# Attention and two MLPs in one kernel: a new order of issue with its own keys for block 1, a fifth `y` buffer, and the output staged in `of`

## The chip, the cores and the metric

One core of one Trainium2 chip (trn2). The metric is device time in microseconds (us). The kernel before takes 1407.87 us, the median of 3 runs (1406.32 to 1409.04).

## The reference

```python
# depthwise softmax-weighted window over 7 positions, 8 heads of 24 channels
w = softmax(weight_gen, axis=-1)                 # (2, 4096, 8, 7), + 1e-9 in the sum
out = einsum('bshk,bskhg->bshg', w, windows(x))  # x (2, 4096, 192), zero-padded by 6
x = out.reshape(8192, 192)
# first MLP
h = x @ w_in                                     # 192 -> 2048
x = (h * sigmoid(h)) @ w_out                     # 2048 -> 192
# second MLP, with a rational activation
h = x @ w_in2
P = a0 + a1 * h + a2 * h * h + a3 * h * h * h
Q = 1 + abs(b0) * abs(h) + abs(b1) * h * h
out = (P / (Q + 1e-6)) @ w_out2
```

The weights come as 64-bit floating-point words, which the kernel itself turns into fp32 high and low parts. All arithmetic is fp32, each product of two matrices being five matmuls over high and low parts.

## The kernel before, in words

The 8192 tokens are cut into 16 blocks of 512 (`NB`). A block goes through three stages: the attention (`M`, `p`, `r`, `a` for each of 4 groups of tokens, and the DMA `AD`), which ends with the transposition `T` into an `h` tile in PSUM and the split `XH0`, `XL0`; **unit 1**, eight times (u = 0 to 7) through the first MLP; and **unit 2**, eight times through the second.

A step of unit 1 is `A`u, ten matmuls into an `h` tile (128x1024, L516); on ScalarE `S`u, the SiLU in place (L553), and `H`u, the high part `g1h` (L557); on VectorE `L`u, the low part `g1l` (L561); then `C`u, ten matmuls from `g1h` and `g1l` into the accumulator (L537 to L541). After `C`7 come `EC` (a copy of half the accumulator into `of`, under the name `e`), `EM` (two matmuls, L577), and the split `XH1` (L489), `XL1` (L493).

A step of unit 2 is `B`u, ten matmuls into an `h` tile; on ScalarE `U`u (`t`, L592) and `V`u (`y`, L596), which both read the `h` tile; on VectorE `u`u (L602) and `w`u (L605), which read it again, and `Y`u (L611); on ScalarE `N`u (L616, Ln) and `G`u (L619, Sigmoid); on VectorE `g`u (L622); `h`u, the high part `g2h`, on POOL, ScalarE or VectorE (a helper, L215, L217, L219); `l`u, the low part `g2l` (L632), on VectorE or POOL; then `D`u, ten matmuls. After `D`7 come `FC` (the accumulator into `of`), `FT` (a transposition into an `h` tile), `FE` (from there to SBUF) and `O`, the DMA to the output (L667).

There are two `h` tiles, shared by `A`, `B`, `T` and `FT`: 18 uses for each block. A use can start when the readers of the use before the last are done. The framework also makes two engines that read one PSUM tile wait for each other, in the order in which they are issued, though both only read: a `V` that is issued between `u` and `w` waits for `u`, and `w` for `V`.

Which order the engines issue in is set by a table, `KEYS`: `Plan.op` gives each operation a key, and `Plan.order` sorts all operations by it; each engine runs its own in that order. A middle block's key is the table's value plus `b * PERIOD`. The first and the last block have keys of their own (`z` and `e` ahead of the name). `ENGINES` says which of the possible engines an operation runs on. Unit 2 of one block is interleaved with unit 1 of the next. At the start 28 chunks of weights are prepared (names `q`: `l` a DMA, `a` on ScalarE, `1` to `4` and mostly `x` on VectorE, L329 to L382), and three further parts of the softmax weights (`s1` to `s3`), which go to DRAM and come back block by block (`AW`, into `aw`).

ScalarE's functions need tables: `S` (SiLU), `N` (Ln) and `G` (Sigmoid) each another one, and the program has an ACT_TABLE_LOAD wherever one follows another; copies, `U` and `V` need none.

Of the kernel before, what the change touches and what calls it, by code (L numbers as in the profile page):

```python
# [37 lines left out]
KEYS = """
    cn:-2654.87 q0O0l:-1091.22 q0O2l:-1019.12 q0O0a:-846.22 q0A0l:-814.6 q0O2a:-791.41 q0A0a:-787.86 q0O01:-777.66
    q0O02:-773.39 q0O03:-728.14 q0O21:-683.64 q0B0l:-641.23 q0O04:-622.79 q0O22:-558.4 q0B0a:-553.51 q0B01:-551.38  # L40
    q0O0h:-534.54 q0O23:-490.66 q0A01:-489.63 q0O24:-458.65 q0A1l:-456.85 q0A02:-443.96 q0O2h:-432.99 cl:-416.6
    q0A1a:-414.24 s0l:-411.67 q0O0x:-411.37 q0A03:-410.2 s0m:-410.01 q0A04:-404.48 zX:-403.47 q0A0h:-401.08 ca:-383.3
    q0O1l:-377.93 s0e:-364.89 q0A11:-364.45 q0B02:-363.26 q0A0x:-362.65 q0O1a:-361.6 q0A2l:-354.79 q0O2x:-345.81
    q0B03:-316.92 q0A12:-309.71 q0B04:-303.11 s0n:-287.19 q0A2a:-276.83 q0B0d:-276.41 q0O11:-275.19 q0B0h:-271.54
    q0A13:-270.4 zM0:-265.19 q0O12:-257.47 q0A21:-246.3 q0A14:-238.64 zp0:-238.19 q0A22:-237.38 zr0:-229.4
    q0A23:-224.88 za0:-219.64 q0O13:-215.26 zM1:-214.13 q0A24:-200.03 q0O6l:-191.2 q0A3l:-175.29 q0A1h:-175.16
    q0A1x:-172.73 q0A3a:-168.08 zp1:-167.7 q0B1l:-164 q0A31:-160.72 q0O6a:-160.16 zr1:-157.97 q0O61:-156.06
    za1:-153.62 q0O62:-150.5 zM2:-148.24 q0O14:-147.91 zp2:-143.67 q0A32:-141.33 q0A2h:-139.04 zr2:-130.1
    q0B0x:-129.28 X:-122.84 za2:-121.15 q0O1h:-119.09 q0O63:-116.78 q0O3l:-114.33 zM3:-113.33 q0B1a:-108.33
    q0O1x:-107.5 zp3:-105.83 q0A33:-104.78 AW:-103.75 zr3:-103.7 M0:-102 q0B11:-99.99 p0:-99.17 q0O64:-98.62 r0:-95.49  # L50
    q0O3a:-95.08 za3:-94.88 q1A0l:-93.71 q0B12:-93.54 q0A34:-92.42 a0:-91.77 q0O31:-91.43 q0O6h:-90.26 M2:-89.49
    q0A2x:-89.37 q0B13:-87.76 zAD:-87.54 q0O32:-85.82 zT:-85.5 zXH0:-84.82 p2:-84.81 r2:-82.87 q0B14:-81.83 s1l:-79.62
# [674 lines left out]
```

## Time and profile before

| | us |
|---|---|
| median of 3 runs | 1407.87 (1406.32 to 1409.04) |
| the profiled execution's own time | 1408.39 |
| its span, first to last instruction | 1406.6 |
| TensorE (PE) busy | 1247.3 (89%) |
| VectorE (DVE) busy | 1144.8 (81%) |
| ScalarE (ACT) busy | 1044.6 (74%) |
| GpSimd (POOL) busy | 586.3 (42%) |

A block's period is read from one `EM` to the next: the sixteen `EM` start at 114.25, 202.64, 286.44, 366.81, 448.46, 528.88, 609.24, 689.59, 769.99, 851.63, 932.01, 1012.36, 1092.76, 1173.06, 1251.98 and 1328.33 us. A period without softmax work is about 80.4 us from `EM` of block 2 on, and one with `s2` or `s3` in it 81.6.

### The profile page before, as it was taken

Reading aid. Unit: us, or ns where it says so; the run is one execution under the profiler, and the core shown is the slowest. Engines: PE = TensorE matmul, PEld = TensorE weight load, DVE = VectorE, ACT = ScalarE, POOL = GpSimd, SP = SyncE. Lnnn points to the kernel's source line nnn. Section 1 sums busy time; section 2 is a strip of 40 time slices with the busy share of each in tenths; the row PEclk is TensorE's granted clock in tenths of the full one; section 3 lists DMA queues with packets and bytes.
Section 4 is the critical chain, followed back from the end, with each engine's and each line's share of the span. In section 5 each row is a group of like instructions: output and inputs, shape, how many; then the busy total and the mean of one; then the engine's idle time right before and its main releaser. Section 6 shows DMA issues by size and latency. Waiting matters only on the chain.

```text
span 1406.6 us, 14510 instructions
## 1 busy us (share of the span) xinstructions
PE 1247.3 (89%) x5472; PEld 1001.1 (71%) x5472; DVE 1144.8 (81%) x1073; ACT 1044.6 (74%) x1000; POOL 586.3 (42%) x328
## 2 busy tenths in 40 slices
...
DMA packets 24294, 45.00 MB, mean 32 GB/s; under 512 B 10404, under 2 KB 16674, under 8 KB 24224
## 3 DMA queue, kind: packets, MB, share of 16 engines
...
q8 instruction: 43, 0.70, 0.2%
q14 instruction: 27, 0.22, 0.1%
...
## 4 chain that ended last, share of the span: by engine, by line
PE 63%; DVE 19%; issue 8%; ACT 7%; DMA 2%; SPq 0%; POOL 0%; DVEq 0%; ACTq 0%; POOLq 0%
PE h L516 33%; PE acc L540 5%; PE acc L537 5%; PE acc L538 5%; PE acc L539 5%; PE acc L541 5%; DVE t L602 5%; DVE t L605 4%; ACT y L596 3%; DVE g1l L561 2%; ACT t L592 2%; DVE y L611 1%; PE acc L577 1%; DMA aw<-wsm 1%; DVE pr L445 1%
## 5 line engine op out<-in xcount | busy, mean ns | idle before, releaser
L516 PE MATMUL h<-xh,wa 128*128 128x512 f32 x1024 | 329.6, 403 | 94.4 <-DVE g1l L561 55.3
L516 PEld LDWEIGHTS h<-xh,wa 128*128 128x128 f32 x1024 | 187.3, 191 | 159.9 <-issue 64.3
L217 POOL TENSOR_SCALAR g2h<-t 128x1024 fp32r<-128x1024 f32 x93 | 119.9, 1289 | 405.7 <-PE acc L539 388.6
L602 DVE TENSOR_TENSOR t<-t,h 128x1024 f32<-128x1024 f32 x128 | 155.4, 1215 | 101.0 <-ACT y L596 48.1
L632 POOL TENSOR_TENSOR g2l<-t,g2h 128x1024 fp32r<-128x1024 f32 x88 | 223.9, 2546 | 22.3 <-ACT g2h L215 14.5
L596 ACT ACTIVATE y<-h,b_sb 128x1024 f32<-128x1024 f32 x128 | 142.5, 1113 | 120.6 <-PE h L516 86.1
L611 DVE SCALAR_TENSOR_TENSOR y<-y,b_sb 128x1024 f32<-128x1024 f32 x128 | 205.2, 1615 | 25.0 <-ACT y L596 24.9
L592 ACT ACTIVATE t<-h,a_sb 128x1024 f32<-128x1024 f32 x128 | 153.9, 1203 | 68.6 <-PE h L516 67.6
L516 PE MATMUL h<-xl,wa 128*128 128x512 f32 x512 | 202.2, 395 | 2.3 <-DVE xl L493 2.3
L561 DVE TENSOR_TENSOR g1l<-h,g1h 128x1024 fp32r<-128x1024 f32 x128 | 156.0, 1219 | 57.4 <-ACT g1h L557 57.3
L516 PE MATMUL h<-xh,wb 128*128 128x512 f32 x512 | 202.3, 395 | 0.0
L516 PE MATMUL h<-xl,wb 128*128 128x512 f32 x512 | 201.5, 394 | 0.0
L622 DVE SCALAR_TENSOR_TENSOR t<-t,a_sb,y 128x1024 f32<-128x1024 f32 x128 | 188.1, 1489 | 2.6 <-ACT y L619 2.5
L436 POOL TENSOR_TENSOR pr<-xw,aw 128x1344 f32<-128x1344 f32 x45 | 139.2, 3093 | 117.9 <-DVE ao L455 117.9
L553 ACT ACTIVATE h<-h 128x1024 f32<-128x1024 f32 x128 | 129.0, 1008 | 62.5 <-PE h L516 59.0
L605 DVE SCALAR_TENSOR_TENSOR t<-t,a_sb,h 128x1024 f32<-128x1024 f32 x128 | 163.7, 1280 | 14.1 <-ACT y L596 9.8
L616 ACT ACTIVATE y<-y,c_sb 128x1024 f32<-128x1024 f32 x128 | 146.6, 1148 | 9.3 <-DVE y L611 8.9
L557 ACT ACTIVATE g1h<-h 128x1024 fp32r<-128x1024 f32 x128 | 130.8, 1023 | 16.7 <-PE acc L539 14.3
L619 ACT ACTIVATE y<-y 128x1024 f32<-128x1024 f32 x128 | 125.9, 1048 | 0.4
L516 PEld LDWEIGHTS h<-xl,wa 128*128 128x128 f32 x512 | 97.5, 190 | 24.7 <-DVE xl L493 3.4
L516 PEld LDWEIGHTS h<-xh,wb 128*128 128x128 f32 x512 | 97.7, 191 | 21.5
L516 PEld LDWEIGHTS h<-xl,wb 128*128 128x128 f32 x512 | 97.4, 190 | 21.3
...
## 6 DMA issues: line engine op xcount, KB each, us to landing
...
raw<-in_moe_w_out_dram SPq DMA_DIRECT2D x16, 384.0 KB, 3.2
out_dram<-o SPq DMA_DIRECT2D x16, 384.0 KB, 5.8
...
```

What stands on the lines that cost most here:

```text
L436: e.tensor_tensor(out=p.rearrange("p k (h g) -> p k h g", g=G), in0=st[xw][:, j:j + K, :].rearrange("p k (h g) -> p k h g", g=G), in1=weig ...
L516: pe.matmul(out=h[:, i], lhsT=w[:, f], rhs=xx, start=(n == 0), stop=(n == len(terms) - 1))
L557: act.activation(out=t, in_=st[hb], func=AF.Copy)
L561: dve.tensor_tensor(out=t, in0=st[hb], in1=st[gh].bitcast(F32), op=ALU.subtract)
L592: act.activation(out=q, in_=st[hb], func=AF.Identity, scale=a_sb[:, 3:4], bias=a_sb[:, 2:3])
L596: act.activation(out=q, in_=st[hb], func=AF.Abs, scale=b_sb[:, 1:2])
L602: dve.tensor_tensor(out=st[t], in0=st[t], in1=flat(), op=ALU.mult)
L605: dve.scalar_tensor_tensor(out=st[t], in0=st[t], scalar=a_sb[:, 1:2], in1=flat(), op0=ALU.add, op1=ALU.mult)
L611: dve.scalar_tensor_tensor(out=st[y], in0=st[y], scalar=b_sb[:, 0:1], in1=st[y], op0=ALU.add, op1=ALU.mult)
L616: act.activation(out=st[y], in_=st[y], func=AF.Ln, scale=c_sb[:, 0:1], bias=1e-6)
L622: dve.scalar_tensor_tensor(out=st[t], in0=st[t], scalar=a_sb[:, 0:1], in1=st[y], op0=ALU.add, op1=ALU.mult)
L632: e.tensor_tensor(out=q, in0=st[t], in1=st[gh].bitcast(F32), op=ALU.subtract)
```

## The change

The tables `KEYS` and `ENGINES` are new throughout; block 1 has keys and engines of its own, under the letter `y`. The `y` tiles (raw weights, and `V`, `Y`, `N`, `G`) get a fifth buffer. The tile `o` is gone: `FE` writes into the `of` tile that `FC` filled, and `O` reads it there.

```diff
 PERIOD = 72.0
 KEYS = """
-    cn:-2654.87 q0O0l:-1091.22 q0O2l:-1019.12 q0O0a:-846.22 q0A0l:-814.6 q0O2a:-791.41 q0A0a:-787.86 q0O01:-777.66
...
+    q0O2l:-2905.19 q0O2a:-2539.72 q0O21:-2364.95 q0B0l:-2204.63 q0O0l:-2184.08 q0A0l:-2133.13 q0O22:-2044.17
...
 ENGINES = """
-    EC:1 FC:1 FE:1 M0:1 a0:1 a1:1 a2:1 eEC:1 eM2:1 ea1:1 ea2:1 eh2:2 eh6:2 eh7:2 el0:1 el1:1 el3:1 ep2:1 ep3:1 er0:1
...
+    EC:1 a1:1 eEC:1 ea1:1 eh0:2 eh1:1 eh3:2 eh5:1 eh6:2 el3:1 el6:1 ep0:1 er0:1 er2:1 h0:2 h1:1 h3:2 h5:1 h6:2 l3:1
...
 BUFS = dict(
-    h=2, acc0=1, acc1=1, xw=1, aw=2, pr=1, ao=1, xh0=1, xl0=1, xh1=1, xl1=1, of=1, o=1,
-    g1h=2, g1l=2, y=4, t=5, g2h=2, g2l=2,
+    h=2, acc0=1, acc1=1, xw=1, aw=2, pr=1, ao=1, xh0=1, xl0=1, xh1=1, xl1=1, of=1,
+    g1h=2, g1l=2, y=5, t=5, g2h=2, g2l=2,
 )
...
-        if b in (0, NB - 1) and name[0] not in "qsc":
-            name = "ze"[b > 0] + name
+        own_key = "" if name[0] in "qsc" else {0: "z", 1: "y", NB - 1: "e"}.get(b, "")
+        name = own_key + name
         engines = engines.split()
         eng = engines[self.engines.get(name, 0)]
-        key = self.keys.get(name, 0.0) + (b * PERIOD if 0 < b < NB - 1 else 0.0)
+        key = self.keys.get(name, 0.0) + (0.0 if own_key else b * PERIOD)
...
         def evac(e):
-            st[o] = t = new("o", [P, JB, D])
+            t = st[of].rearrange("p a c -> p (a c)")[:, 0:JB * D].rearrange("p (j d) -> p j d", d=D)
+            st["o", b] = t
             round_to(e, t, st[tp][:, :, 0:D])
 
         def store(e):
-            sp.dma_start(out=out_t[:, JB * b:JB * (b + 1), :], in_=st[o])
+            sp.dma_start(out=out_t[:, JB * b:JB * (b + 1), :], in_=st["o", b])
...
-        plan.op("FE", b, "ACT DVE", evac, rd=[(*tp, 0)], wr=[(*o, 0)])
-        plan.op("O", b, "SP", store, rd=[(*o, 0)])
+        plan.op("FE", b, "ACT DVE", evac, rd=[(*tp, 0)], wr=[(*of, 0)])
+        plan.op("O", b, "SP", store, rd=[(*of, 0)])
```

In a middle block `FC` and `FE` move from VectorE to ScalarE; `M`0, `a`0 and `a`2 from VectorE to POOL; `l`0, `l`1, `l`2, `l`4 and `l`5 from POOL to VectorE and `l`6 the other way; `h`0, `h`3 and `h`6 from ScalarE or POOL to VectorE, `h`1 from POOL to ScalarE. Lines of the changed kernel are 27 or 28 higher from `Plan` on: L553 is L580, L596 is L623, L592 is L619, L616 is L643, L619 is L646.

**The first place** is ScalarE in a middle block, around `S` and `H` of unit 1. Before, twelve rows in a row, `V`0, `U`0, `S`3, the load for Ln, `N`0, `H`3 and so on:

```order
L596 ACTIVATE y<-h,b_sb 128x1024
L592 ACTIVATE t<-h,a_sb 128x1024
L553 ACTIVATE h<-h 128x1024
L616 ACT_TABLE_LOAD
L616 ACTIVATE y<-y,c_sb 128x1024
L557 ACTIVATE g1h<-h 128x1024
L616 ACTIVATE y<-y,c_sb 128x1024
L596 ACTIVATE y<-h,b_sb 128x1024
L592 ACTIVATE t<-h,a_sb 128x1024
L596 ACTIVATE y<-h,b_sb 128x1024
L616 ACTIVATE y<-y,c_sb 128x1024
L592 ACTIVATE t<-h,a_sb 128x1024
```

With the change, another such stretch, `G`, `S`, `H`, `V`, `U`, `N`, `N`, `S`, `H`:

```order
L646 ACT_TABLE_LOAD
L646 ACTIVATE y<-y 128x1024
L580 ACT_TABLE_LOAD
L580 ACTIVATE h<-h 128x1024
L584 ACTIVATE g1h<-h 128x1024
L623 ACTIVATE y<-h,b_sb 128x1024
L619 ACTIVATE t<-h,a_sb 128x1024
L643 ACT_TABLE_LOAD
L643 ACTIVATE y<-y,c_sb 128x1024 x2
L580 ACT_TABLE_LOAD
L580 ACTIVATE h<-h 128x1024
L584 ACTIVATE g1h<-h 128x1024
```

The three functions alternate more often: where six loads stood in a middle block, there are now fifteen, and 236 in the program instead of 114. `V` now stands ahead of `U` in all steps of a middle block but one; the printed waits of the program count 31 `w` that wait for ScalarE before and none after, and 53 `V` that wait for VectorE before and 20 after.

**The second place** is VectorE at the start, where the first two low parts of block 0 (`g1l`) stand against the first multiplication of block 1 (`pr<-xw,aw`), which needs softmax weights that go through DRAM. Before:

```order
L335 TENSOR_SCALAR dec<-dec 128x512
L347 SCALAR_TENSOR_TENSOR dec<-raw,dec 128x512
L378 TENSOR_TENSOR wo_84<-dec,wo_84 128x2x64
L382 TENSOR_TENSOR wo_84<-dec,wo_84 128x2x128
L341 SCALAR_TENSOR_TENSOR dec<-raw,dec 128x512
L436 TENSOR_TENSOR pr<-xw,aw 128x1344
L347 SCALAR_TENSOR_TENSOR dec<-raw,dec 128x512
L561 TENSOR_TENSOR g1l<-h,g1h 128x1024
```

With the change:

```order
L368 SCALAR_TENSOR_TENSOR dec<-raw,dec 128x512
L374 SCALAR_TENSOR_TENSOR dec<-raw,dec 128x384
L374 SCALAR_TENSOR_TENSOR dec<-raw,dec 128x512
L356 TENSOR_SCALAR dec<-dec 128x384
L588 TENSOR_TENSOR g1l<-h,g1h 128x1024 x2
L362 TENSOR_SCALAR dec<-dec 128x384
L356 TENSOR_SCALAR dec<-dec 128x384
L368 SCALAR_TENSOR_TENSOR dec<-raw,dec 128x384
L362 TENSOR_SCALAR dec<-dec 128x384
L463 TENSOR_TENSOR pr<-xw,aw 128x1344
```

The multiplication moved from ahead of the first `g1l` to behind the first two. Also, 102 rows instead of 77 now stand ahead of the first `xl` on VectorE; the rows added are weight preparation.

**The third place** is VectorE around `EC`, the copy into `e`, in a middle block, with the semaphores that each row waits for (DMAHW is a DMA). Before:

```order
L436 TENSOR_TENSOR pr<-xw,aw 128x1344 [waits DMAHW5_49,DMAHW4_49]
L611 SCALAR_TENSOR_TENSOR y<-y,b_sb 128x1024 [waits Activation_49]
L602 TENSOR_TENSOR t<-t,h 128x1024 [waits PE_49,Activation_49]
L605 SCALAR_TENSOR_TENSOR t<-t,a_sb,h 128x1024 [waits DVE_49]
L493 TENSOR_TENSOR xl_1724<-tp,xh_1703 128x1024 [waits Activation_49]
L219 COPY e<-acc_1283 128x512 [waits PE_49]
L219 COPY o<-to 128x768
L449 TENSOR_TENSOR pr<-pr 128x384 [waits Pool_49]
L622 SCALAR_TENSOR_TENSOR t<-t,a_sb,y 128x1024 [waits Activation_49]
```

With the change:

```order
L629 TENSOR_TENSOR t<-t,h 128x1024 [waits PE_49,Activation_49]
L632 SCALAR_TENSOR_TENSOR t<-t,a_sb,h 128x1024 [waits DVE_49]
L638 SCALAR_TENSOR_TENSOR y<-y,b_sb 128x1024
L588 TENSOR_TENSOR g1l<-h,g1h 128x1024 [waits PE_49,Activation_49]
L520 TENSOR_TENSOR xl_5004<-tp,xh_4989 128x1024 [waits Activation_49]
L659 TENSOR_TENSOR g2l<-t,g2h 128x1024 [waits Pool_49]
L649 SCALAR_TENSOR_TENSOR t<-t,a_sb,y 128x1024 [waits Activation_49] x2
L246 COPY e<-acc_4551 128x512 [waits DMAHW0_49,PE_49]
L246 CAST g2h<-t 128x1024 [waits DVE_49]
```

`EC` of block b+2 now waits for a DMA as well: `O` of block b, which reads the same `of` tile; `FE` is no longer behind `EC` but on ScalarE ahead of it.

## Rows read from the trace of the kernel before

**Rows 1.** The page, part 1: busy us, share of the span and instructions of each engine.

```profile
PE 1247.3 (89%) x5472; PEld 1001.1 (71%) x5472; DVE 1144.8 (81%) x1073; ACT 1044.6 (74%) x1000; POOL 586.3 (42%) x328
```

**Rows 2.** Six stretches, EM to EM: length, busy of each engine, clock, DMA share, GB/s.

```profile
0.00:114.25 114.25, 47.61 (x187) 36.40 (x187) 86.48 (x151) 44.50 (x62) 24.73 (x24) 0.94 0.51 141
114.25:202.64 88.39, 70.02 (x281) 53.73 (x280) 72.05 (x86) 69.13 (x68) 29.51 (x27) 0.95 0.16 47
202.64:286.44 83.80, 76.16 (x333) 60.21 (x332) 72.77 (x66) 68.26 (x65) 35.36 (x22) 0.99 0.07 20
609.24:689.59 80.35, 76.67 (x343) 62.02 (x342) 65.75 (x57) 61.90 (x59) 37.31 (x19) 1.00 0.07 21
769.99:851.63 81.64, 76.70 (x343) 62.02 (x342) 72.25 (x63) 65.51 (x62) 37.35 (x19) 1.00 0.11 35
1328.33:1406.61 78.28, 58.15 (x237) 45.02 (x235) 58.92 (x48) 52.31 (x47) 23.58 (x13) 0.91 0.03 11
```

**Rows 3.** Chain that ended last, 85 to 130 us: start, length, what.

```profile
90.00 2.28 PE h L516 x10
```

**Rows 4.** Waits in 609.24 to 689.59: engine line <- awaited: total us, times, longest.

```profile
PE h L516 <- DVE g1l L561: 2.7, 2, 1.6
PE h L516 <- DVE t L605: 1.0, 2, 0.6
ACT y L596 <- PE h L516: 6.2, 4, 2.3
ACT t L592 <- PE h L516: 4.5, 3, 2.7
ACT h L553 <- PE h L516: 3.0, 2, 2.5
DVE t L602 <- ACT y L596: 3.7, 1, 3.7
ACT y L596 <- DVE t L602: 2.0, 2, 1.3
```

**Rows 5.** Groups by line, 609.24 to 689.59: xcount | busy, mean ns | idle.

```profile
L553 ACT ACTIVATE h<-h 128x1024 f32<-128x1024 f32 x8 | 8.1, 1008 | 3.3 <-PE h L516 3.0
L592 ACT ACTIVATE t<-h,a_sb 128x1024 f32<-128x1024 f32 x8 | 9.6, 1203 | 4.5 <-PE h L516 4.5
L596 ACT ACTIVATE y<-h,b_sb 128x1024 f32<-128x1024 f32 x8 | 8.9, 1114 | 8.2 <-PE h L516 6.2 <-DVE t L602 2.0
L602 DVE TENSOR_TENSOR t<-t,h 128x1024 f32<-128x1024 f32 x8 | 9.7, 1215 | 7.7 <-ACT y L596 3.7 <-ACT t L592 2.4 <-PE h L516 1.6
L605 DVE SCALAR_TENSOR_TENSOR t<-t,a_sb,h 128x1024 f32<-128x1024 f32 x8 | 10.2, 1281 | 0.3
L632 DVE TENSOR_TENSOR g2l<-t,g2h 128x1024 fp32r<-128x1024 f32 x2 | 2.4, 1215 | 0.0
```

**Rows 6.** Groups by line over the whole span, four on ACT and DVE.

```profile
L616 ACT ACT_TABLE_LOAD x38 | 48.8, 1283 | 0.7
L219 DVE CAST g2h<-t 128x1024 fp32r<-128x1024 f32 x5 | 3.4, 689 | 0.2
L341 DVE SCALAR_TENSOR_TENSOR dec<-raw,dec 128x384 int32<-128x384 int32 x16 | 11.6, 725 | 0.0
L335 DVE TENSOR_SCALAR dec<-dec 128x384 int32<-128x384 int32 x16 | 5.6, 352 | 0.1
```

**Rows 7.** Timeline of DVE, 50 to 80 us: start, us, instruction [idle before].

```profile
52.87 1.22 DVE L493 TENSOR_TENSOR xl<-tp,xh 128x1024 fp32r<-128x1024 f32 x1
71.31 1.56 DVE L436 TENSOR_TENSOR pr<-xw,aw 128x1344 f32<-128x1344 f32 x1 [5.39 <-DMA aw<-wsm]
73.38 1.22 DVE L561 TENSOR_TENSOR g1l<-h,g1h 128x1024 fp32r<-128x1024 f32 x1
```

**Rows 8.** DMA issues at 576 us and at 1172 us: KB, us to landing.

```profile
out_dram<-o SPq DMA_DIRECT2D x1, 384.0 KB, 5.9
...
out_dram<-o SPq DMA_DIRECT2D x1, 384.0 KB, 2.3
```

More of the change, by code (lines that the diff above doesn't have):

```diff
@@ L44 @@
[L44 to L48, printed above, removed]
@@ new lines @@
+    q0A1x:-934.468 q0O3a:-914.202 q0A2l:-907.534 q0O6h:-899.202 q0A34:-888.41 q0O6x:-869.054 q0O31:-865.516
+    q0B0h:-863.986 q0A3h:-850.71 q0A2a:-819.632 q0B0x:-812.113 q0O32:-799.318 q0O1l:-794.677 q0O4a:-774.134
+    q0O41:-772.826 zM0:-767.396 q0O33:-764.402 q0O42:-751.111 zp0:-746.658 q0B1l:-732.284 q0B1a:-732.232
+    q0O43:-722.978 q0B11:-715.493 q0A3x:-707.93 q0B12:-701.62 zr0:-700.724 q0B13:-680.396 q0O44:-676.965
+    q0B14:-655.214 q1A0l:-649.35 q0O1a:-648.426 za0:-644.669 q0O34:-640.153 q0A21:-639.628 q0O11:-633.508 zM1:-628.129
@@ new lines @@
+    q0O3h:-604.626 q0O4h:-600.879 q0O3x:-600.432 zp1:-595.135 q0O4x:-588.616 zr1:-581.259 q0A22:-569.147
+    q0O7l:-564.253 q1B0l:-560.522 za1:-557.432 q1A0a:-553.063 q1A01:-548.259 q0B1d:-544.254 zM2:-530.032
+    q0O12:-527.092 q1A02:-516.212 q1B0a:-515.075 zp2:-505.96 q1A03:-505.423 zr2:-503.073 q0A23:-494.477 za2:-488.171
+    q0A24:-484.23 q0O5l:-470.932 q1B01:-466.26 zM3:-464.786 q1A04:-460.6 q0B1h:-455.591 zp3:-452.341 q0B1x:-451.635
+    q1B02:-447.734 q1A0h:-447.649 q0O5a:-445.238 zr3:-444.525 q0A2h:-435.629 q1B03:-426.559 q1A0x:-421.243
```

172 lines of the change are left out of this document (97 added, 75 removed).

## Prediction

> **What bounds the kernel now.** I read the page's busy times first: TensorE is busy for 1247.3 of 1406.6 us and no other engine comes near [rows 1], so the question is where its other 159 us lie. The table by stretches, cut from one EM to the next, tells that [rows 2]. Ahead of the first EM TensorE is busy for 47.61 of 114.25 us: 67 us idle. The next two stretches leave 18.4 and 7.6 us. A middle block, as that from 609.24, has 76.67 of 80.35 us: 3.7 idle, and it recurs twelve times from EM of block 2 to EM of block 14 (two of them with softmax work, as the row of 81.64 us). The last stretch, from the last EM, leaves 20.1 us.
>
> In a middle block the table of waits names what TensorE waits for: 2.7 us for g1l (L) and 1.0 for t (w) [rows 4], which is all of the 3.7. Both are the last readers of an h tile. There are two such tiles, so a run of ten matmuls, 2.28 us [rows 3], starts only when the chain on the tile two uses back is through: S, H (about as long), L, or V, U, u, w, at 1.008, 1.0, 1.22 and 1.114, 1.203, 1.215, 1.281 us [rows 5, 7]. The same table shows the two engines waiting for each other over that tile: VectorE 3.7 us for a V that it doesn't use, ScalarE 2.0 us with V behind a u [rows 4].
>
> **The change, by its parts.** The sum is against the profiled execution, 1408.39 us, which is 0.5 above the median.
>
> *Loads in a middle block.* Nine more table loads, 15 for 6, at 1.283 us each with next to nothing idle beside them, 0.7 us in 38 [rows 6], are 11.5 us; FC and FE arrive at about 1.0 and 0.8 (FC passes over a whole tile as S does, 1.008 [rows 5], and FE over three quarters of one). ScalarE goes from 61.90 [rows 2] to some 75.3 us a block. It waits for TensorE for 13.7 us a block now, in three groups [rows 4], so the loads have room there, but only if the block stays at about 80 us. VectorE loses M0 at 1.56 [rows 7], FC and FE at about a tile pass each (1.2 and 0.9) and two short adds (0.35 each), some 4.4 us, and gains four g2l at 1.215 and three g2h at 0.689 [rows 5, 6], 6.9: about 68 of 80. POOL falls from 37 to about 28. TensorE's 76.67 stay. So no engine's sum is over 76.7, and two are within 2 us of each other.
>
> *The order in a middle block.* With V ahead of U, w waits for no V and u for none that comes after U; the 3.7 and 2.0 us go. I walked one block through the new order by these durations. Three places stay late. A1 waits for L0, which on VectorE stands behind EC, h3, g4 and p2: 0.8. A3 needs w0: TensorE gets there 11 runs after EM (0.9 + 0.8 + 11 x 2.28 = 26.8), while B0 ends near 20.0, V0 and U0 at 22.3, and behind u0 VectorE does Y3 and h6 ahead of w0, ending at 26.8 if nothing on POOL slows them and a us later if it does: 0 to 1.0, taken as 1.0. A4 needs L3: 0.3. The SiLU steps are late by one to three us, since a load of 1.28 stands ahead of seven of them, but C steps of earlier tiles fill that. So 76.7 + 2.1 = 78.8 us, against 80.4: 1.6 us a block. Bounds: 76.7 (no wait) and 84 (below).
>
> *EC behind O.* EC now waits for FE, the issue of O and its landing. The trace shows a landing of 5.9 us behind the big load of x that is issued just ahead of it, and of 2.3 us alone [rows 8]. In the new order the x load goes out some 50 us earlier, so 2.3 is the nearer row. FE ends near 72.5 of the block, O is down at 75, EC is over at 75.7, and TensorE has A0 and B7 to do until 78: nothing. At 5.9 it would be 1.3 us a block.
>
> *The twelve middle blocks.* Ten at 1.6 are 16. In the two with softmax work, VectorE would have 68 + 6.5 (72.25 against 65.75 [rows 2]) = 74.5 of 80: I give back 1.5 in each. Together **-13**.
>
> *The start.* VectorE is the bound there: 86.48 busy of 114.25, and ahead of the first xl at 52.87 [rows 2, 7] it does 77 instructions. 102 stand there with the change. The 25 more are mostly steps of weight preparation, at 0.352 to 0.725 us [rows 6]; at about 0.51, the mean of their four kinds, that is 12.8 us, so xl starts at about 66. Behind it the first g1l waits now for a DMA (5.39 us idle ahead of pr, which stands in front of it) until 73.38 [rows 7]; afterwards it is free of that but has 11 us of weights and softmax ahead of it: about 77 for its start. From there on both orders hold TensorE to VectorE's pace; the first EM comes at about 118 instead of 114.25: **+3.5** (0 to +8).
>
> In the next stretch the weights done earlier are missing: instruction by instruction in the new order, VectorE has some 58 us of work for 72.05 [rows 2], TensorE 63 for 27 runs and the rest, ScalarE some 72 with its loads. It took 88.39; I take 78: **-10** (73 by a walk like the one above, 85 if ScalarE's waits stay). The stretch after it has the same 31 runs as a middle block and took 83.80; block 1's own order lets it go as a middle block does, 79: **-5** (0 to -7).
>
> *The end.* The order of block 15 is the middle blocks', less what belongs to a next block. The stretch ahead of the last EM I leave as it is: 0. In the last, 20 us idle are spread over B steps that follow one another, each waiting for V, U, u, w of the tile two back; a walk gives 76.3 for 78.28: **-2** (-5 to +6).
>
> Sum: 1408.4 - 13 + 3.5 - 10 - 5 - 2 = 1381.9, and 0.5 less on the median's scale: **1382 us**. A change under 0.2% (2.8 us) can't be told from none here.
>
> **The rivals.**
> 1. *ScalarE becomes the bound (slower).* Its 75.3 us are in order, and each load stands ahead of an S or N that others wait for. Now it waits 13.7 us a block for TensorE [rows 4]; if the pairing over two tiles keeps 8 of them, a block takes 83.3, 2.9 more: twelve give +35, and with the start's -13.5 that is 1430. It decides from where more than 6 us of waiting stay (80.4 + 1.1 - 75.3). For it: ScalarE and TensorE then both lack slack. Against: my walk leaves ScalarE 3 to 4 us.
> 2. *Only the start gains.* The waits over h tiles pass from L to w, and a block stays at 80.4; or O lands at 5.9 and takes 1.3 of the 1.6. Then 1392 to 1398.
> 3. *No wait is left*: blocks at 77.0, 3.4 less in twelve: 1351.
> 4. *Each switch costs a drain too.* In the rows a load is followed at once: 0.7 us idle in 38 [rows 6]. If each of the fifteen cost as much again, ScalarE would have 94.5 us a block, and twelve blocks 14 us more each: over 1560.
>
> The Trainium skill, "ScalarE: Activation LUTs", section "What ACT_TABLE_LOAD costs", has such a drain, about 1.38 us beside the 1.283 of the load; by it this change would be a clear loss. The rows agree on the load and show no drain, so the sum goes without it.
>
> **How the numbers follow.** The forecast, 1366 to 1391, has 0.40; rival 2 0.19; rival 3 0.11; rival 1 0.20; rival 4 0.02; 0.08 is left for gains at the start and losses in the blocks that cancel. Faster: 0.40 + 0.19 + 0.11 = 0.70; slower 0.22; same 0.08. Both signs hold much, so beside the likeliest case's own range the full one goes from 1352, near rival 3, to 1420, half-way into rival 1, which leaves out about one in six.
>
> **What would show it.** Right: middle blocks of 78 to 80 us by EM, ScalarE busy for 74 to 77 us in them, TensorE's idle time there under 3 us; V's waits for u nearly gone; EM of block 2 at 270 to 277 instead of 286.44; EC waiting for TensorE, not for a DMA. Wrong: blocks over 81 with TensorE waiting for L or T behind ScalarE's loads (rival 1), a first EM past 125, or a wait of EC for O.

## The result, and the profile after

The changed kernel takes **1365.89 us**, the median of 4 runs (1363.69 to 1366.98), against 1407.49 for the kernel before in 4 runs (1406.32 to 1409.04): a ratio of 0.9702, with a 95% interval of 0.9685 to 0.9719. It is faster by 41.6 us; the prediction said 1382, 16 us above what was measured. The profiled execution took 1366.98 us, 41.4 less than the profiled one of before.

The page of the changed kernel, part 1, busy time of each engine (before: [rows 1]):

```profile
PE 1247.4 (91%) x5472; PEld 1000.9 (73%) x5472; DVE 1141.3 (84%) x1111; ACT 1221.6 (89%) x1154; POOL 406.1 (30%) x258
```

TensorE has the same work. ScalarE has 177 us more of it, GpSimd 180 less, and VectorE 38 instructions more in 3.5 us less.

Where the 41.4 us come from is read as before, from one EM to the next:

| stretch | before | after | difference | forecast |
|---|---|---|---|---|
| to the first EM | 114.2 | 130.8 | +16.5 | +3.5 |
| EM 0 to 1 | 88.4 | 70.2 | -18.1 | -10 |
| EM 1 to 2 | 83.8 | 76.4 | -7.4 | -5 |
| EM 2 to 14 (ten plain blocks, two with softmax work) | 965.5 | 935.1 | -30.4 | -13 |
| EM 14 to 15 | 76.3 | 73.6 | -2.7 | 0 |
| from the last EM | 78.3 | 79.0 | +0.8 | -2 |

The first row differs from one execution to another. Four kernels of the experiments below (2, 5, 8 and 9) issue the changed kernel's order up to the first EM, and in their profiles it comes at 127.50, 127.84, 128.66 and 123.70 us; in two with the order of before (3 and 4) it comes at 112.59 and 113.75. The other rows repeat to some 0.2 us where an experiment altered nothing in them.

The same stretches of the changed kernel (length, busy time of each engine, clock, DMA share, GB/s), to be set against [rows 2]. The fourth is the block with `s2`, the fifth a plain one:

```profile
0.00:130.78 130.78, 50.67 (x187) 38.61 (x188) 100.88 (x179) 50.76 (x74) 16.29 (x27) 0.96 0.53 149
130.78:201.03 70.25, 66.05 (x281) 50.96 (x280) 58.83 (x63) 65.32 (x63) 39.73 (x23) 1.00 0.06 18
201.03:277.42 76.39, 74.63 (x333) 60.01 (x332) 66.65 (x63) 72.08 (x67) 23.20 (x16) 1.00 0.07 22
355.19:439.17 83.98, 78.81 (x344) 62.94 (x342) 74.97 (x66) 77.91 (x73) 25.99 (x15) 0.98 0.10 34
592.54:669.39 76.85, 76.54 (x344) 62.03 (x342) 64.98 (x59) 74.83 (x70) 24.83 (x15) 1.00 0.07 22
1286.17:1365.20 79.03, 59.99 (x247) 45.37 (x246) 61.29 (x53) 61.95 (x57) 16.83 (x9) 0.95 0.03 10
```

The plain block is 76.85 us long with TensorE busy for 76.54, so TensorE's own work fills it. Its waits, to be set against [rows 4]:

```profile
DVE g1l L588 <- ACT g1h L584: 8.4, 8, 2.2
DVE t L629 <- ACT t L619: 2.3, 2, 1.3
ACT h L580 <- PE h L543: 0.9, 1, 0.9
ACT y L643 <- DVE y L638: 0.3, 1, 0.3
PE h L543 <- DVE g1l L588: 0.2, 1, 0.2
DVE e L246 <- DMA out_dram<-of: 0.2, 1, 0.2
```

ScalarE waited 13.7 us for TensorE before, and waits 0.9 now; 12.9 us more of work, most of it loads, went into that room. TensorE's 3.7 us of waiting are 0.2. The groups by line over the whole span, after (busy, mean ns of one | idle before), show the loads of one line and the two steps of VectorE whose mean changed:

```profile
L580 ACT ACT_TABLE_LOAD x88 | 112.9, 1283 | 7.8 <-PE h L543 5.4 <-issue 0.8
...
L638 DVE SCALAR_TENSOR_TENSOR y<-y,b_sb 128x1024 f32<-128x1024 f32 x128 | 175.3, 1370 | 1.7 <-ACT y L623 1.6
L649 DVE SCALAR_TENSOR_TENSOR t<-t,a_sb,y 128x1024 f32<-128x1024 f32 x128 | 163.3, 1292 | 4.9 <-ACT y L646 4.9
```

The same two in the kernel before:

```profile
L611 DVE SCALAR_TENSOR_TENSOR y<-y,b_sb 128x1024 f32<-128x1024 f32 x128 | 205.2, 1615 | 25.0 <-ACT y L596 24.9
L622 DVE SCALAR_TENSOR_TENSOR t<-t,a_sb,y 128x1024 f32<-128x1024 f32 x128 | 188.1, 1489 | 2.6 <-ACT y L619 2.5
```

`Y` and `g` are the same instructions in both kernels; 256 of them are 54.7 us shorter now. That is one reason why VectorE is no busier, though it took over eight steps of a block and gave up six.

### The profile page after: what moved, and what is told of

It reads as the page before. It is cut to its first block, busy times and chain, and to the rows that moved or that the text cites. A ratio compares the mean times of both kernels' runs of the same rounds, so it can differ in the third digit from the quotient of the medians.

```text
span 1365.2 us, 14477 instructions
## 1 busy us (share of the span) xinstructions
PE 1247.4 (91%) x5472; PEld 1000.9 (73%) x5472; DVE 1141.3 (84%) x1111; ACT 1221.6 (89%) x1154; POOL 406.1 (30%) x258
## 4 chain that ended last, share of the span: by engine, by line
PE 57%; ACT 24%; DVE 12%; issue 4%; DMA 2%; SPq 1%; POOL 0%; POOLq 0%; DVEq 0%; ACTq 0%
PE h L543 30%; PE acc L567 5%; PE acc L568 5%; PE acc L564 5%; PE acc L565 5%; PE acc L566 5%; ACT y L646 4%; ACT L580 3%; ACT g1h L584 3%; ACT h L580 3%; DVE g1l L588 3%; ACT y L643 2%; ACT t L619 2%; ACT L646 2%; ACT L643 1%
## 5 line engine op out<-in xcount | busy, mean ns | idle before, releaser
L543 PE MATMUL h<-xh,wa 128*128 128x512 f32 x1024 | 328.9, 403 | 30.2 <-DVE t L632 12.8
L463 POOL TENSOR_TENSOR pr<-xw,aw 128x1344 f32<-128x1344 f32 x56 | 156.0, 2786 | 130.4 <-DVE ao L482 65.1
L638 DVE SCALAR_TENSOR_TENSOR y<-y,b_sb 128x1024 f32<-128x1024 f32 x128 | 175.3, 1370 | 1.7 <-ACT y L623 1.6
L649 DVE SCALAR_TENSOR_TENSOR t<-t,a_sb,y 128x1024 f32<-128x1024 f32 x128 | 163.3, 1292 | 4.9 <-ACT y L646 4.9
L619 ACT ACTIVATE t<-h,a_sb 128x1024 f32<-128x1024 f32 x128 | 154.0, 1203 | 2.0 <-PE h L543 1.1
L580 ACT ACTIVATE h<-h 128x1024 f32<-128x1024 f32 x128 | 129.2, 1010 | 28.4 <-PE h L543 27.4
L643 ACT ACTIVATE y<-y,c_sb 128x1024 f32<-128x1024 f32 x128 | 144.2, 1148 | 5.1 <-DVE y L638 4.3
L623 ACT ACTIVATE y<-h,b_sb 128x1024 f32<-128x1024 f32 x128 | 141.9, 1109 | 7.0 <-PE h L543 4.3
L659 POOL TENSOR_TENSOR g2l<-t,g2h 128x1024 fp32r<-128x1024 f32 x37 | 92.5, 2500 | 183.5 <-DVE g2h L246 183.2
L244 POOL TENSOR_SCALAR g2h<-t 128x1024 fp32r<-128x1024 f32 x50 | 55.5, 1110 | 292.5 <-DVE t L649 268.1
L646 ACT ACTIVATE y<-y 128x1024 f32<-128x1024 f32 x128 | 131.9, 1056 | 0.9
L659 DVE TENSOR_TENSOR g2l<-t,g2h 128x1024 fp32r<-128x1024 f32 x91 | 123.9, 1362 | 1.3 <-POOL g2h L244 1.2
```

The source lines that it names most:

```text
L463: e.tensor_tensor(out=p.rearrange("p k (h g) -> p k h g", g=G), in0=st[xw][:, j:j + K, :].rearrange("p k (h g) -> p k h g", g=G), in1=weig ...
L543: pe.matmul(out=h[:, i], lhsT=w[:, f], rhs=xx, start=(n == 0), stop=(n == len(terms) - 1))
L580: act.activation(out=st[hb], in_=st[hb], func=AF.Silu)
L619: act.activation(out=q, in_=st[hb], func=AF.Identity, scale=a_sb[:, 3:4], bias=a_sb[:, 2:3])
L638: dve.scalar_tensor_tensor(out=st[y], in0=st[y], scalar=b_sb[:, 0:1], in1=st[y], op0=ALU.add, op1=ALU.mult)
L643: act.activation(out=st[y], in_=st[y], func=AF.Ln, scale=c_sb[:, 0:1], bias=1e-6)
```

## The experiments

Four explanations of the blocks were open: the waits between `V` and `u`, `w` (theory 1, the prediction's own); the fifth `y` buffer; the moves of `h` and `l` between engines; and VectorE's queue, in which an `L` that TensorE needs stands behind a step of unit 2 (theory 3). The first and the last can be done to the kernel before by moving two to four keys of a middle block. Experiments 1 to 5 and 8 to 10 are one execution each, 6, 11 and 12 four and 7 ten; the four of the changed kernel lie within 3.3 us of each other.

**1. V first, alone.** On the kernel before, each `V` that stood behind its `U` goes just ahead of it (in a middle block these four; 11 more in the first and last block):

```diff
-    V2:60.06 V4:101.67 V5:91.14 V6:106.73
+    V2:59.6 V4:99.17 V5:85.64 V6:103.94
```

> The kernel before, with one change: each V is issued just ahead of its U, so that no w and no u waits for a V that stands behind it. Theory 1 (the waits between the two readers of an h tile made the middle block long): a middle block falls from 80.4 us to 78.8 or less, the total to 1385 or less. Theory 2 (it is the rest of the new order, or the engines on which h and l run): a middle block stays within 80.0 to 80.8, the total within 1402 to 1412.

Measured: 1416.08 us beside 1409.22 for the kernel before, a little more than either theory had. A plain block takes 81.42 us, 1 more than before (some 82.8). Of the stretches between two EMs only that from EM 0 to EM 1 gains by more than half a us, 80.62 for 88.40. The waits of TensorE and the longest of ScalarE in the block from 606.55:

```profile
PE h L516 <- DVE g1l L561: 3.6, 2, 2.5
PE h L516 <- DVE t L605: 0.9, 2, 0.4
...
ACT y L596 <- PE h L516: 13.0, 7, 5.1
```

So ScalarE's waits for `u` are gone, and TensorE waits for 4.5 us instead of 3.7. Why nothing is gained is worked out from [rows 5, 7]: behind a run of `B`, the chain to the last reader is `U`, `u`, `V`, `w` in the one order and `V`, `U`, `u`, `w` in the other. These are the same four instructions, 1.11 + 1.20 + 1.22 + 1.28 = 4.8 us. In the traces `w`2 and `w`6 end 4.8 to 4.9 us behind their run in both kernels; `w`5 and `w`4, which have another step between `u` and `w` on VectorE, end 0.5 and 0.8 us later with `V` first. A wait that vanished from the table had only changed its place in a chain that got no shorter.

Why the block even gets longer shows on VectorE: `u`4 now stands behind both `V`4 and `U`4 and starts 57.8 us into the block instead of 56.7, and `L`6 (L561) stands behind it; TensorE's wait for that `L` is the one of 2.5 us, where the longest was 1.6.

```profile
664.40 1.22 DVE L602 TENSOR_TENSOR t<-t,h 128x1024 f32<-128x1024 f32 x1 [2.72 <-PE acc L541]
665.54 1.22 DVE L561 TENSOR_TENSOR g1l<-h,g1h 128x1024 fp32r<-128x1024 f32 x1
```

From EM 0 to EM 1 the chain does get shorter. There `V`5 stood 5.6 us behind the end of `U`5 in ScalarE's queue, and `w`5 ended 13.6 us behind its run; with `V` first it ends 7.1 behind it.

**2. V first, taken back out of the changed kernel.** `U` and `V` exchange keys wherever `V` stood first, in the middle blocks and the last (seven pairs in each), as here:

```diff
-    V0:73.174 U0:73.88
+    U0:73.174 V0:73.88
```

> The changed kernel, with U ahead of V again in the middle blocks and in the last. u then waits for V as well, 1.1 us more on VectorE's way to w, seven times a block. Theory 1: middle blocks go from 76.9 to 78.5 us or more, the total to 1385 or more. Theory 2: middle blocks stay under 77.5 us, the total under 1375.

Measured: 1385.4 us, as theory 1 had it, but plain blocks of 78.0 us (+1.15), between the two theories; the stretch from EM 2 to EM 3 takes 81.75 (+4.0) and the tail 83.0 (+4). In the block from 596.11 TensorE's wait is one:

```profile
PE h L543 <- DVE t L632: 1.0, 1, 1.0
```

The timeline of VectorE there shows its cause. `Y`3 stands ahead of `w`0 in VectorE's queue and waits 0.98 for `V`3, which `U`3 now precedes; `w`0 ends 0.8 us later than in the changed kernel:

```profile
620.01 1.29 DVE L638 SCALAR_TENSOR_TENSOR y<-y,b_sb 128x1024 f32<-128x1024 f32 x1 [0.98 <-ACT y L623]
621.21 0.69 DVE L246 CAST g2h<-t 128x1024 fp32r<-128x1024 f32 x1
621.81 1.27 DVE L632 SCALAR_TENSOR_TENSOR t<-t,a_sb,h 128x1024 f32<-128x1024 f32 x1
```

V first is worth 1.15 us a block here, through what waits in VectorE's queue. The pair by itself was worth nothing in the blocks of experiment 1.

**3. The fifth buffer alone.** The kernel before, with `y=5`, the output staged in a `y` tile instead of `o` (`o` doesn't fit beside the fifth buffer), and `O` issued right behind `FE`:

```diff
-    h=2, acc0=1, acc1=1, xw=1, aw=2, pr=1, ao=1, xh0=1, xl0=1, xh1=1, xl1=1, of=1, o=1,
-    g1h=2, g1l=2, y=4, t=5, g2h=2, g2l=2,
+    h=2, acc0=1, acc1=1, xw=1, aw=2, pr=1, ao=1, xh0=1, xl0=1, xh1=1, xl1=1, of=1,
+    g1h=2, g1l=2, y=5, t=5, g2h=2, g2l=2,
...
-            st[o] = t = new("o", [P, JB, D])
+            st[o] = t = new("y", [P, W2], name="o")[:, 0:JB * D].rearrange("p (j d) -> p j d", d=D)
```

> The kernel before with five y buffers; to make room, the output is staged in a y tile instead of its own, and O is issued right behind FE. If the fifth buffer itself carries a part of the gain, middle blocks fall by 0.5 us or more from 80.4; if it is only what lets the new order be issued at all, they stay within 80.0 to 80.9 and the total within 1400 to 1414.

Measured: 1405.92 beside 1407.13, blocks of 80.35 to 80.4. By itself the buffer gives nothing. The new order with four buffers was not tried.

**4. Two L's ahead in VectorE's queue.** On the kernel before, `L`6 goes ahead of `u`4 and `L`3 ahead of `g`7; no other operation moves on any engine:

```diff
-    L6:28 g7:143.28
+    L6:27.99 g7:145.4
```

> The kernel before with two low parts moved on VectorE alone: L6 ahead of u4 instead of behind it, and L3 ahead of g7 instead of behind it. Theory 3 (TensorE's 3.7 us a block are mostly two L that stand behind operations of unit 2 in VectorE's order, 1.6 and 1.1 us): a middle block falls from 80.4 to 78.0 to 79.2 us and the total to 1378 to 1394. Theory 4 (the lateness only passes to the next reader of an h tile): the block stays at 79.8 us or more.

Measured: **1381.13** beside 1407.13: 26 us from two places in a queue. Plain blocks take 77.85 instead of 80.35. VectorE's timeline in the kernel before has both places. `L`3 (L561) behind `g`7 (L622), and `L`6 behind a `u`4 (L602) that had itself waited 2.42 for its `U`:

```profile
633.80 2.07 DVE L622 SCALAR_TENSOR_TENSOR t<-t,a_sb,y 128x1024 f32<-128x1024 f32 x1
635.79 1.21 DVE L561 TENSOR_TENSOR g1l<-h,g1h 128x1024 fp32r<-128x1024 f32 x1
...
665.91 1.22 DVE L602 TENSOR_TENSOR t<-t,h 128x1024 f32<-128x1024 f32 x1 [2.42 <-ACT t L592]
667.05 1.22 DVE L561 TENSOR_TENSOR g1l<-h,g1h 128x1024 fp32r<-128x1024 f32 x1
```

The timeline of TensorE has a wait of 1.1 us behind the first of these `L` and one of 1.6 behind the second: the 2.7 us for `g1l` in [rows 4]. With the keys moved, the waits for `g1l` are gone and those for `w` are left (the same block, waits of TensorE):

```profile
PE h L516 <- DVE t L605: 1.5, 3, 0.6
```

**5. h and l on the engines of before.** The changed kernel, with the ten `h` and `l` that it had moved in a middle block, and those of the last, put back:

```diff
-    h0:2 h1:1 h3:2 h6:2 l6:1
+    h0:1 l0:1 l1:1 l2:1 l4:1 l5:1
```

> The changed kernel with g2h and g2l of the middle and last blocks on the engines of the kernel before (six l on POOL instead of two, h mostly on POOL). If the moves from POOL to VectorE carry the gain, middle blocks go back to 79 us or more; if the order does, they stay under 78, VectorE falling from 65 to about 60 us busy a block and POOL rising to about 37.

Measured: 1383.29 us, plain blocks 77.87 (+1.0), blocks with softmax work 86.07 and 85.68. So the order carries most of the gain of a block, and the moves 1.0 us of it. GpSimd is busy for 40.20 us a block instead of 24.83, and TensorE waits for two `L` again:

```profile
PE h L543 <- DVE g1l L588: 1.5, 2, 0.9
```

VectorE was expected to fall to about 60 us a block, since it has seven steps fewer (52 for 59). It stays at 64.65 for 64.98: its other steps got longer. Over the whole span `g`, the same 128 instructions, takes 1.745 us in the mean instead of 1.292 in the changed kernel:

```profile
L649 DVE SCALAR_TENSOR_TENSOR t<-t,a_sb,y 128x1024 f32<-128x1024 f32 x128 | 221.1, 1745 | 16.0 <-ACT y L646 15.8
```

**6. Both parts on the kernel before.** The keys of experiments 1 and 4 together:

```diff
-    V2:60.06 V4:101.67 V5:91.14 V6:106.73 L6:28 g7:143.28
+    V2:59.6 V4:99.17 V5:85.64 V6:103.94 L6:27.99 g7:145.4
```

> The kernel before with two parts of the change put together and nothing else of it: on VectorE the two L steps ahead of u4 and g7 (alone 77.85 us a block, from 80.35), and V issued just ahead of the U of its unit wherever it stood behind (alone 81.4 a block). The output tile, the four y buffers and the engines of h and l are those of before. If the V-first waits pay once the two L are out of the queue, as taking them out of the changed kernel suggests (1.15 us a block), the plain blocks take 76.7 to 77.1 us, the stretch from the first EM to the second some 81 us as with V first alone, and the time is 1358 to 1368 us, all that the change reached. If what V first is worth hangs on the rest of the new order (h and l moved off VectorE, the fifth y buffer), the plain blocks stay at 77.8 to 79 us and the time is 1372 to 1385.

Measured: 1369.86 us, a ratio of 0.9733 (0.9717 to 0.9749). The first expectation missed: plain blocks stay at 77.8, with three waits for `w` of 0.4 us. The second is right on the blocks and too high on the time, since V first gives 6.6 us from EM 0 to EM 1 (81.53 against 88.14 in experiment 4). So the two parts reach all but some 4 us of the changed kernel's time, with a first EM at 115.5 for 130.8, yet not its blocks. VectorE's timeline there has two places that the changed kernel has not:

```profile
611.93 2.74 DVE L611 SCALAR_TENSOR_TENSOR y<-y,b_sb 128x1024 f32<-128x1024 f32 x1 [0.77 <-ACT y L596]
...
621.90 4.78 DVE L611 SCALAR_TENSOR_TENSOR y<-y,b_sb 128x1024 f32<-128x1024 f32 x2
```

GpSimd runs an `M` beside each, and that `M` is stretched as well, to 3.5 us where one with less beside it takes 2.57:

```profile
597.11 2.57 POOL L436 TENSOR_TENSOR pr<-xw,aw 128x1344 f32<-128x1344 f32 x1
...
610.04 3.54 POOL L436 TENSOR_TENSOR pr<-xw,aw 128x1344 f32<-128x1344 f32 x1 [2.87 <-DVE ao L455]
...
622.13 3.47 POOL L436 TENSOR_TENSOR pr<-xw,aw 128x1344 f32<-128x1344 f32 x1 [3.44 <-DVE ao L455]
```

**7. The last microsecond.** Experiment 6, and three operations besides:

```diff
-    C1:-3.35 D5:146.2 Y1:75.56
+    C1:-8.71 D5:144.31 Y1:76.31
```

> The kernel before with both L first and V first, and three operations moved besides: on TensorE C1 ahead of B0 and D5 ahead of B3, on VectorE Y1 behind w3. In the kernel with the two parts alone TensorE waits 0.4 us three times in a block: B0 for w2, A4 for w3, A7 for w4. The chain V, U, u, w behind a run of B is 1.11 + 1.20 + 1.22 + 1.28 = 4.8 us, and only two runs of 2.27 us stand between B2 and B0 and between B4 and A7; ahead of w3 stands Y1, which GpSimd's M beside it stretches to 3.4 us. If the last microsecond of a block is this (two runs are shorter than the chain, one slow Y in front), the waits ahead of B0 and A4 go, that ahead of A7 stays, the plain blocks take 76.9 to 77.2 us and the time is 1357 to 1363 us: the blocks of the changed kernel with GpSimd as busy as before and six table loads a block. If GpSimd's load itself holds the block at 77.85, as three kernels with 37 to 40 us of GpSimd work show the same period, the blocks stay at 77.7 to 78.2 and the time within 3 us of 1370.

Measured: 1410.83 us, a ratio of 1.0013 (1.0003 to 1.0023): neither expectation. The two waits that were to go did go: `A`4, the sixteenth run of the block, ends 37.30 us behind EM instead of 38.69. But a new one came behind it (waits of TensorE in the block from 683.41):

```profile
PE h L516 <- DVE g1l L561: 3.2, 2, 2.9
PE h L516 <- DVE t L605: 0.4, 1, 0.4
```

Since `Y`1 ends later, `N`1, which needs it, starts on ScalarE at 35.9 us of the block instead of 33.6; four `G` and then `S`4 and `H`4 stand behind it, and `L`4 starts 2.0 us later, too late for `A`5. The edit moved a step on VectorE and left out the queue of the engine that waits for it. That the chain's length against the runs between sets the last microsecond is shown for the two waits named; that a block of 77 us can be had on this order is not.

**8. No Sigmoid table.** The changed kernel with `G` as a plain copy (the division by `Q` in unit 2 is then left out, and with it the loads for Sigmoid and some of those that follow it):

```diff
-            act.activation(out=st[y], in_=st[y], func=AF.Sigmoid, scale=-1.0)
+            act.activation(out=st[y], in_=st[y], func=AF.Copy)
```

> The changed kernel with the Sigmoid replaced by a copy, which needs no table: 125 table loads instead of 236 (the second MLP's activation is not computed). Theory A (the loads lie in ScalarE's spare time): middle blocks stay at 76.5 to 76.9 us with ScalarE busy for about 63 instead of 74.8, and the total falls by under 12 us, all of it in the start, the two softmax blocks and the end. Theory B (ScalarE's loads hold TensorE up): the total falls by over 20 us.

Measured: 1353.87 us, 13 less than the profiled execution of the changed kernel, with ScalarE busy for 65.71 us a block instead of 74.83. A plain block takes 76.41, of which TensorE is busy for 76.39. So 111 loads fewer, some seven a block, give 0.45 us a block; the rest of the 13 comes from the softmax blocks (82.5 and 81.1), the stretches up to EM 2 and the end. Of it 2.1 us are the first EM at 128.66, which lies within what that row varies by.

**9. Three more loads a block.** The changed kernel with `FC`, `h`5 and `XH0` of the middle blocks computing an exponential instead of a copy, so that each needs a table (the values of these three are changed by it), as in `XH0`:

```diff
-            act.activation(out=t, in_=st[tp], func=AF.Copy)
+            act.activation(out=t, in_=st[tp], func=AF.Exp if m == 0 and 2 < b < NB - 1 else AF.Copy)
```

> The changed kernel with three more table loads in each middle block: FC, one h and XH0 run as Exp instead of a copy on ScalarE (so the values are not the kernel's). ScalarE goes from 74.8 to 78.7 us a block, with 76.9 us to lie in. If ScalarE is the next bound in line, blocks take 78.7 to 79.8 us and the total is 1387 to 1403; if loads still lie in waiting time, blocks stay under 77.6 us and the total under 1378.

Measured: 1409.59 us, plain blocks of 80.9. The stretch of a plain block in this kernel (columns as above):

```profile
599.20:680.17 80.97, 77.19 (x344) 61.95 (x342) 64.98 (x59) 78.82 (x73) 24.81 (x15) 1.00 0.07 21
```

And TensorE's waits in it:

```profile
PE h L543 <- DVE g1l L588: 1.6, 1, 1.6
PE h L543 <- DVE t L632: 1.1, 1, 1.1
PE acc L564 <- ACT of L683: 0.9, 1, 0.9
```

4.0 us more of ScalarE's time make the block 4.1 longer: nothing of them is hidden, and both numbers are above either expectation. By ScalarE's sum alone the block could have been 78.8 us; ScalarE is idle for 2.15 of its 80.97 us, as it was for 2.02 of 76.85. So its steps in their order bound this block next. These three loads stand ahead of steps that TensorE needs (the 0.9 us are a wait for `FC` itself); whether three loads at other places would have cost as much was not tried.

**10. The start.** `zX` and `zXL0` (the load of the raw activations, and the first `xl`) ahead of what had stood in front of them:

```diff
-    zX:-992.585 zXL0:-287.361
+    zX:-1440.0 zXL0:-310.753
```

> The changed kernel with two keys changed: the load of x for block 0 is issued ahead of the seventh load of weights, where SyncE waits for a y buffer anyway, and the first xl goes ahead of the softmax part s1 on VectorE, which waits 4.8 us for its DMA. If the first EM is late for these two waits (6.6 and 4.8 us idle on VectorE), it comes at 118 to 125 us instead of 130.8 and the total falls by 5 to 12 us; if VectorE's work sets it whatever the waits, it moves by less than 3 us.

Measured: 1362.85 us, 3 less; the first EM comes at 126.40, 4.4 earlier than in the profile of the changed kernel, all else as there. Both lie between the two expectations. But the profiles with the start left as it was have the first EM at 123.70 to 130.78, so no gain is shown by this one execution. What did move is the first `xl`, to 63.98 from 73.91 (69.32 at the earliest in the others), and it did not take the first EM with it. The timeline of VectorE in the changed kernel shows what this edit goes around, a softmax step that waits for its load with the first `xl` (L520) behind it, and further down what it does not, a `pr` of block 1 that waits 4.45 us. The view names no releaser for it; its softmax weights, issued at 83.33 us with 2.1 to landing, had long come, and the last piece of its load of `x`, issued at 84.48 behind them in SyncE's queue, lands at 93.07:

```profile
71.05 1.32 DVE L299 TENSOR_REDUCE sm<-sm 128x160 f32<-128x1120 f32 x1 [4.83 <-DMA sm<-in_weight_gen_dram]
...
73.91 1.20 DVE L520 TENSOR_TENSOR xl<-tp,xh 128x1024 fp32r<-128x1024 f32 x1
...
93.15 1.56 DVE L463 TENSOR_TENSOR pr<-xw,aw 128x1344 f32<-128x1344 f32 x1 [4.45 <-issue]
```

**11. The start, with softmax work first.** `s1` whole goes ahead of the first `M`, and `zX` as in experiment 10:

```diff
-    zX:-992.585 s1l:-346.022 s1m:-310.743 s1e:-280.568 s1n:-271.88 s1s:-224.596
-    q0B1l:-732.284 zM0:-767.396 zp0:-746.658 zr0:-700.724
+    zX:-1440.0 s1l:-1170 s1m:-945 s1e:-905 s1n:-780 s1s:-778
+    q0B1l:-782 zM0:-715 zp0:-701 zr0:-690
```

> The changed kernel with its start in another order, by the table alone: the load zX at once behind the first weights, and the softmax part s1 (load, top, exp, norm, store) ahead of the first M instead of between M3 and AD, while the tile it needs is free. Nothing behind the first EM is touched. If the first EM of the changed kernel is late (130.8 us) because two transfers stood in its way (raw activations loaded late behind a weight wait, s1m waiting for its load with the L steps of the first block behind it), the first EM comes at 118 to 123 us, all later spacings stay (plain blocks 76.85, softmax blocks 84.0 and 82.3), and the time is 1354 to 1360 us. If the start is set by the weight preparation itself (transposes and evictions, of which there are as many as before), the first EM stays at 125 to 131 us and the time at 1361 to 1367.

Measured: **1353.93 us** (1352.28 to 1354.87), a ratio of 0.9612 (0.9594 to 0.963): the lowest of the kernels here that compute the reference, 12 us below the changed kernel's median, and the two intervals of the ratio lie apart. The first EM comes at 119.13, which is 4.6 to 11.7 earlier than in the five profiles with the other start; the spacings behind it stay, but for the block with `s2` (82.55 for 83.98) and the tail (some 77.1 for 79.03). Ahead of it VectorE is busy for 99.39 us instead of 100.88, and idle for 19.7 instead of 29.9 (25.0 in the earliest of the five). So what the new start saves is idle time and not work: the waits of 4.83 and 4.45 us are gone, and one of 1.5 for the store of `s1` has come.

**12. Softmax work in smaller pieces.** Experiment 11, and the parts from `s2` on held in `y` tiles, 16 groups each, with two operations split in two:

```diff
-NR = 20
+NR = 16
...
-        buf = ("aw", 0) if keep else ("pr", "sm", j0)
+        buf = ("aw", 0) if keep else ("pr" if j0 == JB else "y", "sm", j0)
...
+        plan.op(name + "t", 0, "DVE", less, rd=tok, wr=tok)
...
+        plan.op(name + "v", 0, "DVE", scale, rd=tok, wr=tok)
```

> The kernel with the new start, and with the later softmax parts made differently: 16, 16, 16 and 12 groups instead of three times 20, held in a tile of the y pool from the second on instead of the single tile that M also needs, and with the subtraction and the final multiplication as operations of their own, so that VectorE is held for shorter stretches and M of the next block on GpSimd waits for nothing of it. There are now three blocks with a softmax part instead of two. If the two softmax blocks lose their 7.1 and 5.5 us because one operation of 4.1 us on VectorE stands ahead of two L steps and because M waits for the shared tile, the three blocks with a part take 77.5 to 79.5 us each, and the time is 8 to 12 us below that of the kernel with the new start alone. If they lose them because VectorE has no room for some 6 us of more work in a block (it is busy 65.0 of 76.85 us), or because the load and the store disturb the block, the three take 81 to 83 us each and the time is the same within 3 us or above.

Measured: 1355.03 us (1351.74 to 1355.46), the same as 11, as the second expectation has it. Three blocks of 81.1, 80.1 and 80.4 us stand where two of 82.5 and 82.3 stood: against plain ones some 11 us in either kernel. The single tile and the long step were not the whole cause, and what else holds a block with softmax work is open.

## Why the prediction was right, and where it was off

**The direction and the range** held; 1366 lies 14 us above the lower end, and at the lower edge of the likeliest case's own 1366 to 1391. That it lies there at all is in part luck: the forecast of the blocks was 17 us too careful and that of the first EM 13 too kind, and the two errors partly cancel. With the first EM as forecast the time would have been some 1353 (an estimate, 1366 less the 13), at the very end of the full range. Of its own signs, the plain blocks lie below the 78 to 80 named for right, and a first EM past 125 is one of those named for wrong.

**The middle blocks** were the term that was mis-sized: 76.85 us where 78.8 were forecast. The walk gave three late places, `A`1 at 0.8, `A`3 at 1.0 and `A`4 at 0.3; in the trace `A`1 waits 0.19, `A`3 nothing, `A`4 0.12. For `A`3 I took the upper end, since GpSimd might slow VectorE ahead of `w`0; GpSimd is busy for 24.83 us a block, not the 28 summed, and there it did not. Rival 3, 77.0 with a chance of 0.11, is what a plain block did (its time, added up from the prediction's own terms, is 1354 and not 1351).

**The reason** was only partly the one given: "With V ahead of U, w waits for no V and u for none that comes after U; the 3.7 and 2.0 us go." They went, but they were waits of VectorE and ScalarE, and 2.7 of TensorE's 3.7 us were for `L`. Experiment 4 gets 2.5 of the 3.5 us a block from two `L` alone, experiment 1 nothing from `V` alone. [Rows 4] told which steps TensorE waits for, and I then explained the gain by two waits that don't end at TensorE. In the stretch from EM 0 to EM 1 `V` first does pay, 7.8 us in experiment 1 and 6.6 in experiment 6, of the 18.1. Of the last 1.0 us of a block, experiments 2 and 5 show that in the new order both V first and the moved `h` and `l` are needed: without either the block is back near 77.9. What moving `M`0, `a`0 and `a`2 to GpSimd and `FC` and `FE` to ScalarE is worth was not tried by itself.

**ScalarE** came out as summed, 74.83 us against 75.3. Rival 1 (83.3 us a block) did not come about: of its 13.7 us of waiting for TensorE 0.9 is left, so the pairing kept nothing. But it was near: in experiment 9 three loads more make a block longer by all that they take.

**No drain** (rival 4). The 39 loads more of experiment 9 raise ScalarE's busy time from 1221.6 to 1273.4, 1.33 us each, and the load itself takes 1.283. Nor does a drain show as idle time: in the block of experiment 9, with 18 loads, ScalarE is idle for 2.15 us in all. The Trainium skill, "ScalarE: Activation LUTs", section "What ACT_TABLE_LOAD costs", adds a drain of about 1.38 us to each load; an estimate from its figures gives the 39 loads some 104 us. The measurement decides: none is seen here.

**EC behind O** waits 0.2 us in a plain block, and TensorE does not wait for `EC`: nothing, as forecast. The landing of 384 KB takes 2.3 us where nothing large goes out ahead of it, in the changed kernel as in [rows 8].

```profile
out_dram<-of SPq DMA_DIRECT2D x1, 384.0 KB, 2.3
```

**The two blocks with softmax work** were to give 1.5 us back each; against a plain block they take 7.1 and 5.5 more. I counted VectorE's room (74.5 of 80; it was 74.97) and not what stands behind the work. In the block of `s2` TensorE waits 5.0 us in three pieces. The chain that ended last, ahead of the longest of them, has a `Y` of 2.45 us, `u` and `w` (start, length, what):

```profile
416.80 2.45 DVE y L638
419.24 1.14 DVE t L629
...
420.41 1.29 DVE t L632
...
421.83 3.32 PE h L543 x7
```

Another 2.3 us are TensorE's own: 78.81 busy for 76.54. Cut into stretches of 4 us, the granted clock falls at that wait:

```profile
415.00:419.00 4.00, 4.00 (x20) 3.28 (x18) 4.00 (x2) 3.97 (x5) 3.84 (x3) 1.00 0.00 0
419.00:423.00 4.00, 1.53 (x5) 1.00 (x4) 3.96 (x5) 3.18 (x4) 1.10 (x1) 0.83 0.00 0
423.00:427.00 4.00, 4.00 (x15) 3.20 (x14) 3.49 (x3) 1.08 (x1) 1.04 (x1) 0.75 0.00 0
427.00:431.00 4.00, 4.00 (x23) 3.39 (x23) 1.68 (x2) 3.94 (x5) 1.79 (x2) 1.00 0.00 0
```

**The start** was the largest miss: the first EM at 130.8 for 118, outside the bound of +8 in all five profiles with this start (123.70 to 130.78). The step that failed is "so xl starts at about 66"; it starts at 73.91. The work was summed rightly: up to the first `xl` VectorE is busy for 51.40 us where it was 38.85, 12.55 more for the 12.8 summed (in 30 instructions more, not 25). The stretch up to the first `xl`, after and before:

```profile
0.00:73.91 73.91, 4.62 (x11) 2.27 (x11) 51.40 (x107) 20.09 (x35) 5.24 (x14) 1.00 0.62 166
0.00:52.87 52.87, 4.62 (x11) 2.27 (x11) 38.85 (x77) 14.54 (x24) 7.95 (x14) 1.00 0.56 158
```

What the sum put at nothing is idle time: 22.5 us instead of 14.0. I had counted VectorE's work and taken for granted that its inputs come no later than before. From `xl` to the first `g1l` it takes 11.2 us, as forecast with 11, and from there to EM 45.7 for 40.9; of these 4.8 us, 3.9 are more work of VectorE. Experiment 11 takes the idle time back in part; which of the waits costs how much is open.

The next stretch gained more than forecast, -18.1 for -10: it goes at 70.25, even below the 73 of the walk. It is no give-back of the late start, since it takes 70.2 to 70.3 us in every profile that leaves its work and order alone, with the first EM at 119.13 as at 130.78. Up to EM 1 the kernel is 1.6 us ahead, where 6.5 were forecast.

**The end** was forecast at 0 and -2, and came at -2.7 and +0.8.
